# First loads and first products of a fused forward and backward pass, in a new order

## The chip, the cores and the metric

The kernel runs on one core of a Trainium2 chip. The time of a run is what the device takes for one launch, in microseconds (us); a version is given by the median of its runs. A profile is one execution recorded by the hardware profiler, with its own time. The engines are TensorE (PE; its weight loads PEld), VectorE (DVE), ScalarE (ACT), GpSimd (POOL) and SyncE (SP), which here only starts DMA transfers. A name with a q (SPq, ACTq) is the engine's sequencer.

## What is computed

A block with two halves, and the gradients of it: a spectral filter and an MLP, each behind a layer norm that six rows of a condition c scale, shift and gate (sa, ca, ga, sb, cb, gb).

```python
mod = (silu(c) @ w_mod).reshape(1, 6, 1, 1024)      # sa, ca, ga, sb, cb, gb
h = layernorm(x) * (1 + ca) + sa                     # x: 1 x 2048 x 1024, bfloat16
x = x + ga * irfft2(rfft2(h) * (w_r + 1j * w_i))
h = layernorm(x) * (1 + cb) + sb
x = x + gb * (gelu(layernorm(h) @ w1 + b1) @ w2 + b2)   # w1: 1024 x 3584
# outputs: x, and the gradients of x, w_r, w_i, w1, b1, w2, b2, c, w_mod for grad_out
```

## The kernel before

The 2048 tokens are four quarters (blocks) of 512, the 1024 columns eight chunks of 128, the 3584 hidden units 28 chunks of 128 (fc).

**Start.** The rows of the condition come from `mod_block(r, h)`: half a row is eight matmuls (L278) of a broadcast u = silu(c) with a 1024 KB piece of w_mod; `mod_get` loads such a piece from SP (L270) into a ring of three tiles. Row 5 is gb, row 1 ca, row 0 sa; rows 2 to 4 are `late_mods`. grad_out is loaded by quarters (`load_go`, L350). Each quarter of it is transposed by 32 matmuls with an identity (L388), scaled by the gb column (`gb_col`, made by small matmuls at L380) and written to `gBoT[j]` by VectorE (L392) and ScalarE (L396) in turn.

**Products with w2^T.** `load_w2t(fc)` loads a transposed chunk of w2 with a transposing DMA (L341) into one of four slots of `wt`. `ph_part(fc, js)` multiplies it with the quarters js of gBoT: eight matmuls (L814) into one bank for each quarter, a copy (L820) to one of four buffers, and a store to d_ph by POOL (L822) when the fourth quarter is done. All 28 fc are needed before the GELU's backward. The first seven are written ahead of the forward transform (`PH_EARLY` = 6 and one more); the others are written behind it, and the scheduler places them as filling between the transform's matmuls; the last four do their quarters 2 and 3 between the first z blocks.

**x and the folds.** `load_tok` loads a quarter of x so that the transform can fold it by symmetry: half its rows plainly from SP (L143), half by two gathers from POOL (L145). Each quarter is normalised (`ln_dve` for the first, `ln_mix` for the others: statistics on VectorE at L489 and L499 and on ScalarE), scaled by 1 + ca and folded along tokens and columns (`fold_tok`, `fold_d`, `fold_pair`, all through the helper at L194), in the buffer `fbuf`. Quarters 2 and 3 of fbuf first hold quarters 2 and 3 of grad_out.

**Forward transform.** `spectral_core` starts with `s_fwd` (matmuls L538 and L531, `pu`), which needs all four folded quarters and is written behind the last early product (`early_pe`). It multiplies by w_r and w_i in pairs of frequencies (`pair_load`, L557 and L558) and goes back; `consume_fwd` makes the two layer norms and stores n3, the MLP's input, by quarters.

**MLP and backward.** `z_block(b, g)` multiplies n3's quarter b with w1 (L951), evicts on ScalarE (L954) and runs the GELU and its derivative on ScalarE and VectorE, in two sets of temporaries. `plan` writes the order of z blocks, the last products (`p`) and the second MLP product (`bo_pass`), and `ordered()` holds TensorE to it. `pg_pass(b, h)` (L1105) makes the gradient at n3: four banks over seven groups g; ScalarE evicts the banks at L1121. The backward transform follows, with `fill(n)` placing n pieces of the weight gradients (16 matmuls each, L1239 and L1464) between its steps, `halves_sum` for column sums (L217), and `colsum` and `sr` for the sa row's gradient.

**What sets the order.** Each engine runs its instructions in the order that the scheduler wrote at build time, from the program's order and priorities. `tc.issue_after(x)` holds what stands under it behind x in that order. SP and POOL start DMAs in order; a DMA that must wait holds those behind it.

Of the kernel before, what the change touches and what calls it, by code (L numbers as in the profile page):

```python
# [10 lines left out]
FP32 = mybir.dt.float32  # L11
BF16 = mybir.dt.bfloat16
# [5 lines left out]
P = 128  # L18
# [12 lines left out]
NB = 4  # L31
# [4 lines left out]
def kernel(  # L36
# [101 lines left out]
    def tok_idx(i, q):  # L138
        return 1 + q if i % 2 == 0 else 3 * q

    def load_tok(t4, src, i, eng=None):
        s3 = tok_flat(src)
        ins = (eng or nc.sync).dma_start(out=tok_plain(t4, i), in_=tok_rows(s3, i, 0, D))  # L143
        for q in range(2):
            nc.gpsimd.indirect_dma_start(out=t4[:, tok_idx(i, q), :], out_offset=None, in_=s3,  # L145
                                         in_offset=bass.IndirectOffsetOnAxis(ap=xidx[:, 2 * i + q:2 * i + q + 1], axis=0))
        return ins
# [201 lines left out]
    def load_go(j):  # L349
        nc.sync.dma_start(out=gos[j], in_=go_f[j * BW:(j + 1) * BW, :].rearrange("(a p) d -> p a d", p=P))  # L350

# [17 lines left out]
    load_tok(x4s[1], A_x, 1)  # L369
    load_go(2)  # L370
    load_go(3)
    for h in range(2):
        mod_block(5, h, wm[5, h][:])
    load_tok(x4s[2], A_x, 2)
    load_tok(x4s[3], A_x, 3)
    load_w2t(2)
    load_w2t(3)
    pc = ps_d("pc")
    for cch in range(NDC):
        nc.tensor.matmul(pc[:, cch:cch + 1], lhsT=gb_row[0:1, cch * P:(cch + 1) * P], rhs=ones_bf[0:1, 0:1], start=True, stop=True)  # L380
    with tc.high_priority():
        nc.vector.tensor_copy(out=gb_col[:], in_=pc[:, 0:NDC])
    for j in range(4):
        for cch in range(NDC):
            pt = ps_f("pt")
            for a in range(4):
                q = (0, 2, 3, 1)[a] if j % 2 == 0 else (1, 3, 2, 0)[a]
                nc.tensor.matmul(pt[:, q * P:(q + 1) * P], lhsT=gos[j][:, a, cch * P:(cch + 1) * P], rhs=(ident, irev)[a // 2],  # L388
                                 start=True, stop=True)
            if cch % 2 == 0:  # L390
                with tc.high_priority():
                    nc.vector.tensor_scalar(out=gBoT[j][:, cch, :], in0=pt[:], scalar1=gb_col[:, cch:cch + 1], scalar2=0.0,  # L392
                                            op0=ALU.mult, op1=ALU.add, accum_out=gu[:, j, cch:cch + 1])
            else:
                with tc.high_priority():
                    nc.scalar.activation(out=gBoT[j][:, cch, :], in_=pt[:], func=ACT.Identity, scale=gb_col[:, cch:cch + 1],  # L396
                                         accum_out=gu[:, j, cch:cch + 1])

# [54 lines left out]
    def gen_mats():  # L453
# [13 lines left out]
        nc.gpsimd.dma_start(out=d_E[:], in_=em1[:])  # L467

    def ln_act(x4, row, i, jk):
        sv = small.tile([P, 4, 4], FP32, tag="lnsv")  # L470
        for q in range(4):
            nc.scalar.activation(out=jk[:, q, :], in_=x4[:, q, :], func=ACT.Identity, accum_out=sv[:, q, 0:1])
        nc.vector.tensor_scalar(out=sv[:, :, 1:2], in0=sv[:, :, 0:1], scalar1=-1.0 / D, scalar2=None, op0=ALU.mult)
        for q in range(4):
            nc.scalar.activation(out=jk[:, q, :], in_=x4[:, q, :], func=ACT.Square, bias=sv[:, q, 1:2], accum_out=sv[:, q, 2:3])
        ln_fin(sv[:, :, 2:3], sv[:, :, 1:2], sv[:, :, 3:4], 1.0 / D, row, i)

# [66 lines left out]
    def spectral_core(fwd, fb, sms, em, css, pt, evac_u, evac_c, evac_v, consume, o4tag, pfs=None, fill=lambda n: None, mid=lambda: None, beside=lambda n, r_in: None):  # L544
# [7 lines left out]
        def pair_load(n):  # L552
            par, m = n // 4, n % 4
            ws = ws2[:, n % 2]
            for x, w in ((0, A_w_r), (1, A_w_i)):
                sl = w_slot(par, m)
                ld_in[0] = (nc.sync if fwd else nc.gpsimd).dma_start(out=ws[:, x, sl, 0:DF], in_=w_plus(w, par, m))  # L557
# [228 lines left out]

    for h in range(2):
        mod_block(0, h)
    gen_mats()
# [7 lines left out]
    to_cols(b1_col[:], b1r, NFC, ident[:])  # L797
    nc.vector.tensor_scalar(out=sar[:, 0], in0=sar[:, 0], scalar1=8.0, scalar2=None, op0=ALU.mult)
    fold_d(saf.rearrange("p (c d) -> p c d", c=1), sar[:, 0], sar[:, 1])


    pho = reg.tile([P, 3, 4, BW], BF16, name="pho", tag="ot")
    phs = [pho[:, k] for k in range(3)] + [reg.tile([P, 4, BW], BF16, name="phr", tag="ph")[:]]
    last_pe = [None]

    def ordered():
        return tc.issue_after(last_pe[0].ins)

    def ph_part(fc, js):
        ph2 = phs[fc % 4]  # L810
        for j in js:
            pp = ps_f("pp")
            for cch in range(NDC):
                last_pe[0] = nc.tensor.matmul(pp[:], lhsT=wt[:, fc % 4, cch, :], rhs=gBoT[j][:, cch, :],  # L814
                                              start=(cch == 0), stop=(cch == NDC - 1))
            q = (0, 2, 3, 1)[j]
            ov = ph2[:, :, q * P:(q + 1) * P]
            pv = pp[:, :].rearrange("p (i w) -> p i w", w=P)
            with tc.high_priority():
                nc.any.tensor_copy(out=ov, in_=pv)  # L820
        if js[-1] == 3:
            nc.gpsimd.dma_start(out=d_ph[fc * P:(fc + 1) * P, :], in_=ph2.rearrange("p i w -> p (i w)"))  # L822

    PH_EARLY = 6
    late_mods = [(r, h) for r in (2, 3, 4) for h in range(2)]
    for fc in range(PH_EARLY):
        ph_part(fc, (0, 1, 2, 3))
        load_w2t(fc + 4)
        if fc in (3, 5):
            with tc.issue_after(last_pe[0].ins):  # L830
                for r, h in late_mods[3 * (fc // 2 - 1):3 * (fc // 2)]:
                    mod_block(r, h)

    ph_part(PH_EARLY, (0, 1, 2, 3))
    early_pe = last_pe[0]

    for i in range(4):
        x4, fb = x4s[i], fbuf[:, i]
        if i == 0:
            with tc.issue_after(u_in.ins):  # L840
                ln_dve(x4, 0, i)
        elif i > 0:
            ln_mix(x4, 0, i, fb)
        else:
            ln_act(x4, 0, i, fb)
        norm_act(fb, x4, 0, i)
# [49 lines left out]
    PH_KEEP = NFC - 4  # L896
    for fc in range(PH_EARLY + 1, NFC):
# [201 lines left out]
    def pg_pass(b, h, pool, before=lambda: ExitStack()):  # L1099
        pgs = [pool(k)("pg") for k in range(4)]  # L1100
        for g in range(7):
            for i in range(4):
                for k in range(4):
                    with before():
                        last_pg[0] = nc.tensor.matmul(pgs[i][:], lhsT=gzs[b, g][:, k, i * P:(i + 1) * P],  # L1105
                                                      rhs=w1Ts[g][:, k, h * KH:(h + 1) * KH],
                                                      start=(g == 0 and k == 0), stop=(g == 6 and k == 3))
                    last_pe[0] = last_pg[0]
                g0 = 3 if b == NB - 1 else 2
                if b > 0 and h == 0 and (g, i) in ((g0, 0), (g0 + 1, 2), (g0 + 2, 2)):  # L1110
                    for ins in sums_in[g - g0]:
                        behind(ins, last_pg[0])
                    sums_in[g - g0].clear()
            for k in range(4 if b < 2 and h == 1 else 0):
                nc.scalar.activation(out=gzs[b, g][:, k, :], in_=gzs[b, g][:, k, :], func=ACT.Identity,
                                     accum_out=gb1_acc[:, g * 4 + k, b:b + 1])
            if g < 6:
                yield
# [253 lines left out]
    def consume_bwd(i, o4, tmp, tmp2, n1, eb):  # L1372
# [198 lines left out]
```

## Time and profile before

| | |
|---|---|
| median of 3 runs | 1411.57 us (1410.99 to 1412.05) |
| the profiled execution | 1412.42 us |
| its span on the core | 1410.6 us |
| TensorE busy | 1374.2 us |
| VectorE busy | 1072.4 us |
| ScalarE busy | 739.2 us |
| GpSimd busy | 351.2 us |
| granted TensorE clock, mean | 0.992 |
| HBM | 200 GB/s over the span |

The span runs from the first to the last recorded instruction; the rest of the execution's time lies around it. "Busy" is the union of an engine's instructions; a matmul's mean duration is longer than its share of a stream, because matmuls overlap. In a group, the number behind x is the count; "idle before" is the time that the engine stood still just ahead of these instructions, and the name behind the arrow is what ended it.

### The profile page before, as it was taken

Reading aid. Unit: us, or ns where it says so; the run is one execution under the profiler, and the core shown is the slowest. Engines: PE = TensorE matmul, PEld = TensorE weight load, DVE = VectorE, ACT = ScalarE, POOL = GpSimd, SP = SyncE. Lnnn points to the kernel's source line nnn. Section 1 sums busy time; section 2 is a strip of 40 time slices with the busy share of each in tenths; the row PEclk is TensorE's granted clock in tenths of the full one; section 3 lists DMA queues with packets and bytes.
Section 4 is the critical chain, followed back from the end, with each engine's and each line's share of the span. In section 5 each row is a group of like instructions: output and inputs, shape, how many; then the busy total and the mean of one; then the engine's idle time right before and its main releaser. Section 6 shows DMA issues by size and latency. Waiting matters only on the chain. (4 is left out here: it accounts for less than half of the span.)

```text
span 1410.6 us, 18696 instructions
## 1 busy us (share of the span) xinstructions
PE 1374.2 (97%) x6963; PEld 664.5 (47%) x6963; DVE 1072.4 (76%) x1507; ACT 739.2 (52%) x1059; POOL 351.2 (25%) x436
## 2 busy tenths in 40 slices
PE   5998999999999999999999999999999999999999
PEld 2545565444444444444444444444544565444444
DVE  5897889987978777887620688999498757979960
ACT  4774667667877765665314583243622444434311
POOL 5510623201112122112210010112345330322341
PEclk8899999999999999999999999999999999999999
DMA  9972666899787777696999499996689996897971
GB/s 330 301 234 57 176 165 200 265 283 350 256 258 242 229 242 249 189 287 224 298 271 232 138 237 321 259 259 209 197 265 288 261 253 173 218 250 189 286 270 38
DMA packets 361265, 333.22 MB, mean 236 GB/s; under 512 B 208026, under 2 KB 303152, under 8 KB 361046
## 3 DMA queue, kind: packets, MB, share of 16 engines
q1 hardware_dynamic: 319990, 206.01, 55.9%
q0 software_dynamic: 35424, 120.78, 24.5%
q10 hardware_dynamic: 5760, 5.25, 1.2%
q8 instruction: 54, 0.88, 0.3%
q14 instruction: 37, 0.30, 0.1%
HBM read 166.77 MB, written 115.92 MB: 200 GB/s over the span
## 5 line engine op out<-in xcount | busy, mean ns | idle before, releaser
L1105 PE MATMUL pg<-w1T,gzr 128*128 128x512 bf16 x896 | 196.0, 379 | 2.8 <-ACT gn3b L1121 2.8
L814 PE MATMUL pp<-gBoT,wt 128*128 128x512 bf16 x896 | 197.9, 380 | 0.8 <-DVE phr L820 0.4
L1464 PE MATMUL gw1acc<-gzh,n3n 128*128 128x512 bf16 x640 | 140.0, 379 | 0.2 <-DVE gwo L1468 0.2
L1105 PEld LDWEIGHTS <-gzr 128*128 128x128 bf16 x896 | 86.6, 98 | 111.1 <-issue 8.5
L1464 PEld LDWEIGHTS <-n3n 128*128 128x128 bf16 x896 | 87.3, 98 | 107.1 <-issue 3.3
L951 PEld LDWEIGHTS <-w 128*128 128x128 bf16 x896 | 87.2, 98 | 107.0 <-issue 2.5
L814 PEld LDWEIGHTS <-wt 128*128 128x128 bf16 x896 | 87.5, 98 | 104.0 <-issue 1.5
L951 PE MATMUL pz<-n3Tb,w 128*128 128x512 bf16 x448 | 99.2, 379 | 1.0 <-DVE w2sD L1027 1.0
L951 PE MATMUL pz<-n3Ta,w 128*128 128x512 bf16 x448 | 98.7, 379 | 0.0
L1005 PEld LDWEIGHTS <-hhA 128*128 128x128 bf16 x608 | 59.0, 98 | 73.1 <-issue 2.8
L1239 PE MATMUL gw2acc<-gB,hhsA 128*128 128x512 bf16 x416 | 92.2, 379 | 0.0
L954 ACT ACTIVATE gt<-pz,b_col 128x512 bf16<-128x512 f32 x112 | 72.8, 683 | 33.2 <-PE pz L951 33.0
L962 ACT ACTIVATE gt<-gt 128x2048 bf16<-128x2048 bf16 x28 | 53.5, 1911 | 64.8 <-DVE gt L194 64.8
L194 DVE TENSOR_TENSOR gt<-gt,gt 128x2048 bf16<-128x2048 bf16 x56 | 68.6, 1224 | 19.8 <-ACT gt L964 18.5
L194 DVE TENSOR_TENSOR ct<-ct 128x2048 bf16<-128x2048 bf16 x68 | 80.6, 1218 | 0.9
L1468 ACT CAST gwo<-gw1acc 128x512 bf16<-128x512 f32 x50 | 28.4, 581 | 89.3 <-PE gw1acc L1464 78.5
L1247 ACT CAST gwo<-gw2acc 128x512 bf16<-128x512 f32 x40 | 23.3, 584 | 93.6 <-PE gw2acc L1239 90.5
L1239 PEld LDWEIGHTS <-hhsA 128*128 128x128 bf16 x416 | 40.7, 98 | 47.4
L1470 POOL DMA_DIRECT2D out_dram<-gwo x53 | 29.2, 554 | 129.8 <-DVE gwo L1468 67.6
L1464 PE MATMUL gw1acc<-gzu,n3n 128*128 128x512 bf16 x256 | 55.6, 379 | 1.2 <-ACT gwo L1468 1.2
L958 ACT ACTIVATE gt<-gt 128x2048 bf16<-128x2048 bf16 x28 | 53.5, 1909 | 2.1 <-DVE hhC L194 1.3
L964 ACT ACTIVATE gt<-gt 128x2048 bf16<-128x2048 bf16 x28 | 53.4, 1907 | 0.4
(347 smaller groups left out, 2558.4 us busy)
## 6 DMA issues: line engine op xcount, KB each, us to landing
gzr<-d_gz SPq DMA_DIRECT2D x28, 512.0 KB
wblk<-in_w_mod_dram SPq DMA_DIRECT2D x12, 1024.0 KB
out_dram<-otl POOLq DMA_DIRECT2D x48, 256.0 KB, 4.9
d_ph<-pho POOLq DMA_DIRECT2D x21, 512.0 KB, 6.0
d_hh<-hhA POOLq DMA_DIRECT2D x19, 512.0 KB, 5.1
w<-in_B_w_dram SPq DMA_DIRECT2D x7, 1024.0 KB
hhC<-d_ph SPq DMA_DIRECT2D x14, 512.0 KB
w2sA<-d_ph SPq DMA_DIRECT2D x14, 512.0 KB
```

Source lines behind the costliest of these rows:

```text
L194: return nc.vector.tensor_tensor(out=out, in0=a, in1=b, op=op)
L814: last_pe[0] = nc.tensor.matmul(pp[:], lhsT=wt[:, fc % 4, cch, :], rhs=gBoT[j][:, cch, :], start=(cch == 0), stop=(cch == NDC - 1))
L951: last_pe[0] = nc.tensor.matmul(pz[:], lhsT=w1s[g][:, cch, k * P:(k + 1) * P], rhs=n3T[:, cch, :], start=(cch == 0), stop=(cch == NDC - 1))
L954: z_in = nc.scalar.activation(out=zb[:, k, :], in_=pz[:], func=ACT.Identity, bias=b1_col[:, fc:fc + 1], scale=1.0)
L958: nc.scalar.activation(out=av, in_=zb, func=ACT.Square)
L962: nc.scalar.activation(out=sg, in_=bv, func=ACT.Sigmoid, scale=2.0 * GK)
L964: nc.scalar.activation(out=bv, in_=bv, func=ACT.Sigmoid, scale=-2.0 * GK)
L1005: last_pe[0] = nc.tensor.matmul(pbs[i][:], lhsT=hh[:, k, i * P:(i + 1) * P], rhs=wp[:, k, :], start=False, stop=(g == 6 and k == 3))
L1105: last_pg[0] = nc.tensor.matmul(pgs[i][:], lhsT=gzs[b, g][:, k, i * P:(i + 1) * P], rhs=w1Ts[g][:, k, h * KH:(h + 1) * KH], start=(g == 0 ...
L1239: nc.tensor.matmul(acc[:], lhsT=hh_of(fc)[:, t, :], rhs=gBs[t // 4][:, t % 4, h * KH:(h + 1) * KH], start=(t == 0), stop=(t == NT - 1))
L1464: nc.tensor.matmul(acc[:], lhsT=n3ns[t // 4][:, t % 4, cch * P:(cch + 1) * P], rhs=gz2[t // 8][:, t % 8, :], start=(t == 0), stop=(t == NT ...
L1470: eng.dma_start(out=out_4[cch * P:(cch + 1) * P, fg * 512:(fg + 1) * 512], in_=ob)
```

## The change

The order of the first loads, and with it of TensorE's first work, is rewritten:

- gb's two pieces, quarter 0 of grad_out and w2^T 0 and 1 are loaded first; then x0, quarter 1, w2^T 2, ca's pieces, quarter 2, x1, quarter 3, x2, w2^T 3, x3, and behind x3 sa's pieces. Each quarter's gathers of x wait until a named quarter of grad_out has landed.
- Each quarter's transposes are followed at once by its products with fc 0, 1 and 2; the ca row is made behind quarter 1. TensorE's order is written out here.
- `PH_EARLY` is 11: fc 3 to 10 follow, with the rows sa, ga, sb, cb between them, and their copies on ScalarE. The loads of rows 2 to 4 wait for a w2^T load.
- All quarters of x use `ln_mix`, each behind the last evictions of a quarter's transposes. The fold of sa moves into the loop of products.
- The first loads of w_r and w_i wait for w2^T 12.
- In `pg_pass`, for b > 0 and h = 0, the groups are taken in the blocks (0, 1), (2), (3), (4, 5, 6): within a block one bank does all its groups before the next bank.
- In `consume_bwd` one piece of filling moves from behind to ahead of the third column sum. `sr` takes another buffer.

```diff
-    def load_tok(t4, src, i, eng=None):
+    def load_tok(t4, src, i, eng=None, landed=None):
...
-            nc.gpsimd.indirect_dma_start(out=t4[:, tok_idx(i, q), :], out_offset=None, in_=s3,
+            got_ = nc.gpsimd.indirect_dma_start(out=t4[:, tok_idx(i, q), :], out_offset=None, in_=s3,
...
+            if landed is not None:
+                tc.add_manual_dep(got_.ins, landed.ins.name, mybir.DependencyInfo(mybir.DependencyClass.Sync, mybir.DependencyReason.DATA),
+                                  reason="loads in turn")
...
-    mod_get(1, 0)
-    load_tok(x4s[0], A_x, 0)
-    mod_get(1, 1)
     mod_get(5, 0)
-    for h in range(2):
-        mod_block(1, h, wm[1, h][:])
     mod_get(5, 1)
-    load_go(0)
+    go_in = [load_go(0)]
     load_w2t(0)
     load_w2t(1)
-    load_go(1)
-    load_tok(x4s[1], A_x, 1)
-    load_go(2)
-    load_go(3)
+    load_tok(x4s[0], A_x, 0, landed=go_in[0])
+    go_in.append(load_go(1))
+    load_w2t(2)
+    mod_get(1, 0)
+    mod_get(1, 1)
+    go_in.append(load_go(2))
+    load_tok(x4s[1], A_x, 1, landed=go_in[2])
+    go_in.append(load_go(3))
+    load_tok(x4s[2], A_x, 2, landed=go_in[3])
+    load_w2t(3)
+    x3_in = load_tok(x4s[3], A_x, 3, landed=go_in[3])
+    for h in range(2):
+        with tc.issue_after(x3_in.ins):
+            mod_get(0, h)
...
     for h in range(2):
         mod_block(5, h, wm[5, h][:])
-    load_tok(x4s[2], A_x, 2)
-    load_tok(x4s[3], A_x, 3)
-    load_w2t(2)
-    load_w2t(3)
...
+    for j in range(4):
+        turn_go(j)
+        for fc in range(3):
+            ph_part(fc, (j,))
+        if j == 1:
+            for h in range(2):
+                with ordered():
+                    mod_block(1, h, wm[1, h][:])
+    for fc in range(3):
+        load_w2t(fc + 4)
...
-                    ld_in[0] = (nc.sync if fwd else nc.gpsimd).dma_start(out=ws[:, x, sl, 0:DF], in_=w_plus(w, par, m))
+                with tc.issue_after(w2ts[12].ins) if fwd else ExitStack():
+                    ld_in[0] = (nc.sync if fwd else nc.gpsimd).dma_start(out=ws[:, x, sl, 0:DF], in_=w_plus(w, par, m))
...
+                with ordered() if fc < PH_EARLY else ExitStack():
+                    last_pe[0] = nc.tensor.matmul(pp[:], lhsT=wt[:, fc % 4, cch, :], rhs=gBoT[j][:, cch, :],
+                                                  start=(cch == 0), stop=(cch == NDC - 1))
...
-                nc.any.tensor_copy(out=ov, in_=pv)
+                (nc.scalar.copy if 3 <= fc < PH_EARLY else nc.any.tensor_copy)(out=ov, in_=pv)
...
-    PH_EARLY = 6
+    PH_EARLY = 11
...
-    for fc in range(PH_EARLY):
+    for fc in range(3, PH_EARLY):
         ph_part(fc, (0, 1, 2, 3))
+        if fc in (4, 6, 8):
+            with ordered():
+                for r, h in ([(0, 0), (0, 1)], late_mods[0:3], late_mods[3:6])[fc // 2 - 2]:
+                    mod_block(r, h, wm[r, h][:])
         load_w2t(fc + 4)
...
-    ph_part(PH_EARLY, (0, 1, 2, 3))
     early_pe = last_pe[0]
...
-        if i == 0:
-            with tc.issue_after(u_in.ins):
-                ln_dve(x4, 0, i)
-        elif i > 0:
+        dv, ac = turned_in[(0, 2, 3, 3)[i]]
+        with tc.issue_after(dv.ins), tc.issue_after(ac.ins):
             ln_mix(x4, 0, i, fb)
...
-        for g in range(7):
-            for i in range(4):
-                for k in range(4):
+        blocks = ((0, 1), (2,), (3,), (4, 5, 6)) if b > 0 and h == 0 else tuple((g,) for g in range(7))
+        steps = [(g, i, i == 3 and g == block[-1] and block) for block in blocks for i in range(4) for g in block]
+        for n, (g, i, ends) in enumerate(steps):
+            for k in range(4):
...
-        fill((4, 7, 6, 8)[i])
+        fill((4, 7, 7, 8)[i])
         halves_sum(accCA[0], tmp, i == 0, i == 3)
-        fill(2)
+        fill(1 if i == 2 else 2)
...
-    sr = reg.tile([P, 2, 1, D], FP32, name="sr", tag="px0")
+    sr = reg.tile([P, 2, 1, D], FP32, name="sr", tag="smb")
```

More of the change, by code (lines that the diff above doesn't have):

```diff
@@ new lines, with ph_part @@
+    turned_in = []
+    pho = reg.tile([P, 3, 4, BW], BF16, name="pho", tag="ot")
+    phs = [pho[:, k] for k in range(3)]
+    PH_EARLY = 11
+    def ph_part(fc, js):
+        ph2 = phs[fc % 4]
+        for j in js:
+            pp = ps_f("pp")
+            for cch in range(NDC):
+                with ordered() if fc < PH_EARLY else ExitStack():
+                    last_pe[0] = nc.tensor.matmul(pp[:], lhsT=wt[:, fc % 4, cch, :], rhs=gBoT[j][:, cch, :],
+                                                  start=(cch == 0), stop=(cch == NDC - 1))
+            q = (0, 2, 3, 1)[j]
+            ov = ph2[:, :, q * P:(q + 1) * P]
+            pv = pp[:, :].rearrange("p (i w) -> p i w", w=P)
+            with tc.high_priority():
+                (nc.scalar.copy if 3 <= fc < PH_EARLY else nc.any.tensor_copy)(out=ov, in_=pv)
+        if js[-1] == 3:
+            nc.gpsimd.dma_start(out=d_ph[fc * P:(fc + 1) * P, :], in_=ph2.rearrange("p i w -> p (i w)"))
@@ L797, with late_get @@
     to_cols(b1_col[:], b1r, NFC, ident[:])
[L798 to L822, printed above, removed]
-    PH_EARLY = 6
-    late_mods = [(r, h) for r in (2, 3, 4) for h in range(2)]
-    for fc in range(PH_EARLY):
+    phs.append(reg.tile([P, 4, BW], BF16, name="phr", tag="ph")[:])
+    late_mods = [(r, h) for r in (2, 3, 4) for h in range(2)]
+    def late_get(n):
+        for r, h in late_mods[n:n + 3]:
+            with tc.issue_after(w2t_in[0].ins):
+                mod_get(r, h)
+    for fc in range(3, PH_EARLY):
         ph_part(fc, (0, 1, 2, 3))
+        if fc in (4, 6, 8):
+            with ordered():
+                for r, h in ([(0, 0), (0, 1)], late_mods[0:3], late_mods[3:6])[fc // 2 - 2]:
+                    mod_block(r, h, wm[r, h][:])
         load_w2t(fc + 4)
[L829 to L832, printed above, removed]
-    ph_part(PH_EARLY, (0, 1, 2, 3))
+        if fc in (4, 6):
+            late_get(3 * (fc // 2 - 2))
+        if fc == 4:
+            nc.vector.tensor_scalar(out=sar[:, 0], in0=sar[:, 0], scalar1=8.0, scalar2=None, op0=ALU.mult)
+            fold_d(saf.rearrange("p (c d) -> p c d", c=1), sar[:, 0], sar[:, 1])
     early_pe = last_pe[0]
@@ L896 @@
     PH_KEEP = NFC - 4
-    for fc in range(PH_EARLY + 1, NFC):
+    for fc in range(PH_EARLY, NFC):
         if fc >= PH_EARLY + 4:
```

64 lines of the change are left out of this document (30 added, 34 removed).

## The prediction

> **What bounds the kernel now.** The page and the waits of TensorE (engine, line, releaser: us in total, times, longest) come first.
>
> ```profile
> span 1410.6 us, 18696 instructions
> PE 1374.2 (97%) x6963; PEld 664.5 (47%) x6963; DVE 1072.4 (76%) x1507; ACT 739.2 (52%) x1059; POOL 351.2 (25%) x436
> ...
> PE pm L278 <- DMA wblk<-in_w_mod_dram: 9.8, 4, 3.9
> PE pu L538 <- DVE fbuf L194: 5.1, 1, 5.1
> PE pg L1105 <- ACT gn3b L1121: 2.8, 1, 2.8
> ...
> PE accCA L217 <- DVE ct L194: 1.6, 1, 1.6
> ```
>
> TensorE is the bound: its idle time is 1410.6 − 1374.2 = 36.4 us in all, so no reordering can win more than that plus what a slow clock costs. Next, where it idles: the busy time by stretches (PE, PEld, DVE, ACT, POOL with counts; granted clock; DMA share; GB/s).
>
> ```profile
> 0.00:20.00 20.00, 8.73 (x21) 3.05 (x22) 7.76 (x24) 6.57 (x9) 16.54 (x44) 0.97 0.92 324
> 20.00:40.00 20.00, 14.09 (x113) 10.11 (x111) 13.19 (x34) 13.25 (x26) 3.98 (x6) 0.67 1.05 351
> ...
> 2.50:22.50 20.00, 11.04 (x34) 4.09 (x35) 7.88 (x23) 5.28 (x8) 14.62 (x28) 0.91 1.05 371
> 40.50:45.00 4.50, 4.21 (x40) 3.25 (x39) 3.89 (x11) 4.50 (x14) 1.38 (x2) 0.77 1.05 156
> ```
>
> 11.3 + 5.9 = 17.2 us of the 36.4 lie in the first 40 us, while the DMA engines are full. So the start is bound by the order of the bytes, not by work. TensorE's order of time says what it did before the forward transform began (start, duration, count; idle before):
>
> ```profile
> 6.25 3.57 PE L278 MATMUL pm<-wblk,u_b 128*128 128x512 bf16 x8 [3.89 <-DMA wblk<-in_w_mod_dram]
> ...
> 37.05 4.20 PE L388 MATMUL pt<-ident,fbuf 128*128 128x128 bf16 x36 [2.26 <-DMA fbuf<-in_grad_out_dram]
> 41.51 2.55 PE L388 MATMUL pt<-ident,fbuf 128*128 128x128 bf16 x28 [0.27 <-ACT gBoT L396]
> 44.04 5.34 PE L814 MATMUL pp<-gBoT,wt 128*128 128x512 bf16 x24
> ...
> 99.97 7.07 PE L814 MATMUL pp<-gBoT,wt 128*128 128x512 bf16 x32
> ...
> 107.10 9.66 PE L814 MATMUL pp<-gBoT,wt 128*128 128x512 bf16 x44
> 121.87 1.46 PE L538 MATMUL pu<-smA,fbuf 128*128 128x256 bf16 x6 [5.11 <-DVE fbuf L194]
> ...
> 128.06 1.22 PE L538 MATMUL pu<-smA,fbuf 128*128 128x256 bf16 x8
> ```
>
> The forward transform (L538) begins at 121.9. The groups of the stretch 0 to 122 (count | busy, mean ns) give what TensorE had done by then:
>
> ```profile
> L814 PE MATMUL pp<-gBoT,wt 128*128 128x512 bf16 x268 | 59.0, 379 | 0.0
> L278 PE MATMUL pm<-wblk,u_b 128*128 128x512 bf16 x96 | 27.0, 441 | 9.8 <-DMA wblk<-in_w_mod_dram 9.8
> ...
> L388 PE MATMUL pt<-ident,go 128*128 128x128 bf16 x64 | 6.9, 284 | 2.1 <-DVE gBoT L392 1.3 <-DMA go<-in_grad_out_dram 0.7
> ...
> L388 PE MATMUL pt<-ident,fbuf 128*128 128x128 bf16 x64 | 6.7, 284 | 2.6 <-DMA fbuf<-in_grad_out_dram 2.3 <-ACT gBoT L396 0.3
> ```
>
> A warm product costs 7.07/32 = 0.221 us, so 96 modulation products should take 21.2, not 27.0. Useful work is 59.0 + 21.2 + 13.6 = 93.8 us, and 121.9 − 93.8 = 28.1 us are lost before the transform.
>
> **The change, part by part: the start.** It reorders loads and products; it adds no matmul. The sizes and the rate fix when each load lands:
>
> ```profile
> wblk<-in_w_mod_dram SPq DMA_DIRECT2D x9, 1024.0 KB
> x<-in_A_x_dram SPq DMA_DIRECT2D x4, 512.0 KB
> go<-in_grad_out_dram SPq DMA_DIRECT2D x2, 1024.0 KB
> ...
> 31.50 10.70 SPq L341 DMA_TRANSPOSE wt<-in_B_w_dram  x2
> ```
>
> 1024 KB at 371 GB/s is 2.83 us; x is half plain, half gathers, 2.83 together. The two transposed w2 loads that sit at the end of SP's 31.50 to 42.20 are the dip to 156 GB/s in 40.5 to 45.0, so I take 2.25 us for one; from below, a quarter of a wblk's bytes, 0.7; from above half of SP's 10.70, 5.3, which however counts the queue ahead. In the new order: first gb half 6.25 (as the first wblk now), second 9.1, grad_out quarter 0 at 11.9, w2^T 0 and 1 at 16.4, x0 and quarter 1 at 22.1, w2^T 2 at 24.3, the ca row at 30, quarter 2 at 32.8, x1 and quarter 3 at 38.5, then x2, w2^T 3, x3 to 46, the sa row to 52.
>
> TensorE follows, now in one written order. gb row 6.25 + 2 × 3.57 = 13.4, its eviction and the column by about 15 (an estimate: two copies of the 0.7 us kind and some small products). A quarter's 32 transposes take 13.6/4 = 3.4: 18.4. Products 0 and 1 (16 × 0.221 = 3.5) end at 22; product 2 waits for 24.3 and ends at 26.1; quarter 1 (3.4 + 5.3) 34.8; ca row (16 × 0.221) 38.3; quarters 2 and 3 are there, 55.7; products 3 to 10 (256 × 0.221 = 56.6) and eight modulation blocks (8 × 1.77 = 14.2) end at 126.5. By then 352 products are done where 268 were: 84 × 0.221 = 18.6 us more work, 4.6 us later. **TensorE's gain is 14.0 us.** With 0.7 for a transposed load product 2 would wait no more, and it is about 16; with 5.3 the first three land at 22.5 and 33.5, and it is about 5.
>
> [...]
>
> [...]
>
> **The fold chain.** The transform needs all four folded quarters of x. Their cost on VectorE (tile fbuf in 0 to 122; the statistics, two groups), what VectorE evicts, and the chain's end:
>
> ```profile
> 0.00:122.00 122.00, 7.22 (x67) 6.32 (x68) 51.06 (x42) 32.52 (x40) 0.93 0.86 263
> ...
> L499 DVE BATCH_NORM_STATS2 st<-x 128x6 f32<-128x512 bf16 x12 | 7.9, 677 | 0.0
> ...
> L392 DVE TENSOR_SCALAR_CACHE_REDUCE gBoT<-pt,gb_col 128x512 bf16<-128x512 f32 x16 | 11.7, 750 | 3.8 <-PE pt L388 3.3
> ...
> L820 DVE CAST pho<-pp 128x512 bf16<-128x512 f32 x9 | 6.1, 681 | 0.0
> ...
> 121.12 0.69 DVE L194 TENSOR_TENSOR fbuf<-fbuf,sb_saf 128x1024 bf16<-128x1024 bf16 x1
> ```
>
> x and the ca row come later than now, so the chain starts at 38.3. From there: 51.1 of folds, 16 statistics × 0.68 = 10.9, half of the transposes' evictions 5.9, and some 10 of rows, tables and small things (an estimate): 78, to 116, with gaps about 121. The copies of products 3 to 10, part of them VectorE's now, go to ScalarE, which is why this fits. So the written order (126.5) decides. The 5.11 us stop before the transform goes, and with it its cold start: six matmuls took 1.46 (0.243), later eight took 1.22 (0.153); 22 of these are 2.0 us. Against now the transform starts 126.5 − 121.9 = 4.6 later and runs through 2.0 sooner: **2.6 us late**, from −4 (everything lands early) to +14 (the chain waits for all loads to 52 and ends near 136).
>
> Queues: the pair weights' loads, and the sa, ga, sb and cb rows, move behind w2^T loads.
>
> ```profile
> 65.40 0.35 SPq L557 DMA_DIRECT2D ws<-in_A_w_r_dram  x1
> ...
> 100.00:120.00 20.00, 16.76 (x79) 7.48 (x77) 19.83 (x22) 9.49 (x15) 1.06 (x2) 1.00 0.25 80
> ```
>
> The pair loads issue near 105 instead of 65, for work after the transform; the DMA engines are a quarter busy there, so I cost them at nothing. Uncovered, the first two pairs' eight loads of 131 KB are 2.8 us. Three modulation loads are 8.5 us and have two rounds of products, 14.2, above them: nothing; uncovered, up to 8.5. x's gathers now wait on POOL for grad_out to land, the last for quarter 3 at 38.5. Behind them stand the table work (ScalarE's sines wait for it) and the first stores of products, due long after; nothing, as long as the tables are there by the transform. The statistics of x1 wait for quarter 2's evictions and those of x2 and x3 for quarter 3's, near 50, while VectorE has x0 in hand: nothing.
>
> **The first z blocks.** What is late next is the end of the forward stage. TensorE reaches z sooner by its lead of 18.6 us, but ScalarE and VectorE are then still at the last quarter:
>
> ```profile
> 222.32 91.68 PE L814 MATMUL pp<-gBoT,wt 128*128 128x512 bf16 x424
> ...
> 323.03 7.07 PE L951 MATMUL pz<-n3Ta,w 128*128 128x512 bf16 x32
> ...
> 344.26 20.88 PE L951 MATMUL pz<-n3Ta,w 128*128 128x512 bf16 x96
> ...
> 326.95 0.17 DVE L507 TENSOR_SCALAR mv<-mv 128x2 f32<-128x2 f32 x1 [1.46 <-ACT ct L506]
> ...
> 334.41 2.29 DVE L194 TENSOR_TENSOR ct<-ct,rows 128x4096 bf16<-128x4096 bf16 x1 [6.42 <-ACT ct L514]
> ...
> 350.00 2.40 ACT L954 ACTIVATE gt<-pz,b_col 128x512 bf16<-128x512 f32 x4
> ...
> 287.00:345.00 58.00, 57.25 (x266) 25.81 (x264) 44.23 (x71) 38.73 (x51) 5.29 (x9) 1.00 1.02 326
> ```
>
> z(0,1), started at 344.26, is evicted only at 350.00, all four banks in a row, when z(0,2) needs them at 344.26 + 7.07 = 351.3: the slack is under a microsecond. So the lead is worth only what ScalarE and VectorE come earlier. VectorE idles 58 − 44.2 = 13.8 us in 287 to 345; with z(0,0) ready near 305 its GELU can use the 6.4 us gap, the 1.5 us one, and some 1 us of product copies that fell earlier: **9 us**. Bounds: nothing (these queues stay in their order) and 16.6 (every gap, and four copies of 0.7).
>
> **The late edits.** The reordered product pass moves the last three groups of a bank together, so each bank's eviction has 12 matmuls ahead of the next bank's, not 4; this covers the 2.8 us wait behind gn3b: 2.4 (0 to 2.8). One piece moved ahead of the third column sum covers the 1.6 us wait: 1.1 (0 to 1.6); if a wait merely moves to the next bank or piece, both lose as much. The other buffer of sr lies beside the last products: nothing.
>
> **Sum.** −9 + 2.6 − 2.4 − 1.1 = −9.9 us. The profiled execution took 1412.4 with 1.8 around its span of 1410.6; the changed span would be 1400.7, 1402.5 with that. It lies 0.8 above the median 1411.6, so the median becomes **1401.7**.
>
> **Rivals.**
> *Lead survives whole* (0.20). The z stage absorbs it: all gaps are used, the transform begins on time. Then TensorE's own sum decides: −14.0 − 2.0 − 3.5 = −19.5, 1392. For it speaks 13.8 us of idle VectorE; against it the eviction at 350.00.
> *Lead lost* (0.13). No gap is used, −3.5 + 2.6 = about −1, 1411. For it: strict engine queues and slack under 1 us now.
> *Fold chain late* (0.20), the other side. The ca row and x2, x3 land behind everything; the chain starts at about 52, ends near 136, and its lateness passes through to z, where the lead is worth nothing extra. +14 − 2 − 3.5 = +8.5, 1420. It decides once the transform starts more than 9 + 3.5 − 2 = about 10 us late net, so after some 134.
> *It doesn't do what it says* (0.06). DMA is full in both orders; if every transposed load stalls the queue 5.3 us, products wait as now, TensorE's gain is about 5, the transform shifts, and 1411 follows.
>
> **How the numbers follow.** Forecast 0.41, own range 1396 to 1408. Two per mille (2.8 us) is about what this kernel's measurement tells from no change. Faster: 0.40 of the forecast, 0.20, and 0.06 of the 1411 cases: 0.66. Slower: the late chain 0.20 and 0.04 of tails; same 0.10. From 1387 to 1420 leaves out some 0.05 below and 0.12 above.
>
> **What would show it.** First transposes near 15 us and L814 products before 24; 352 products before the first L538; that L538 with no wait on fbuf, at 122 to 130, at full clock; a new wait of TensorE at L951 of some 10 us, released by ScalarE's evictions; gn3b and accCA gone from the waits. Wrong: a wait of L538 on fbuf past 134, or L814 waits on wt in the first 60 us of more than 5 us.

## The result and the profile after

| | before | after |
|---|---|---|
| median | 1411.57 us (1409.44 to 1412.94, 7 runs) | 1422.77 us (1418.23 to 1429.11, 7 runs) |
| ratio to before, 95% interval | | 1.0081 [1.0057, 1.0104] |
| span of the profiled execution | 1410.6 us | 1423.9 us |
| TensorE idle in the span | 36.4 us | 47.8 us |

The change makes the kernel 11.2 us slower; the forecast was 9.9 us faster. In the changed code the w2^T load is L344 and its product L423 (copied at L429), n3's first load L952, the loads of w1 L909, the store of n3 L895, the z block L967 with its eviction L970, the transform L574.

TensorE's waits in the changed kernel (engine, line, releaser: us in total, times, longest):

```profile
PE pp L423 <- DMA wt<-in_B_w_dram: 15.6, 5, 7.9
PE pz L967 <- ACT gt L970: 6.8, 3, 4.5
PE pm L281 <- DMA wblk<-in_w_mod_dram: 3.8, 1, 3.8
PE pp L423 <- DVE pho L429: 3.7, 1, 3.7
PE pg L1122 <- DMA gzr<-d_gz: 3.7, 2, 3.0
```

The old waits on fbuf, gn3b and accCA are gone and those on wblk are shorter. On top stands one that was not there: the products wait for w2^T. Its two long stops, ahead of 24.88 and of 305.24, stand in TensorE's order of time (start, duration, count; idle before):

```profile
24.88 3.59 PE L423 MATMUL pp<-gBoT,wt 128*128 128x512 bf16 x8 [6.44 <-DMA wt<-in_B_w_dram]
...
40.44 1.06 PE L400 MATMUL pt<-ident,fbuf 128*128 128x128 bf16 x16
...
52.94 2.31 PE L400 MATMUL pt<-ident,fbuf 128*128 128x128 bf16 x20 [1.78 <-DVE pho L429]
55.04 6.28 PE L423 MATMUL pp<-gBoT,wt 128*128 128x512 bf16 x24
...
130.63 1.04 PE L574 MATMUL pu<-smA,fbuf 128*128 128x256 bf16 x8
...
305.24 5.72 PE L423 MATMUL pp<-gBoT,wt 128*128 128x512 bf16 x16 [7.86 <-DMA wt<-in_B_w_dram]
...
322.97 7.07 PE L967 MATMUL pz<-n3Ta,w 128*128 128x512 bf16 x32
...
340.68 8.52 PE L423 MATMUL pp<-gBoT,wt 128*128 128x512 bf16 x32 [3.73 <-DVE pho L429]
...
364.45 7.07 PE L967 MATMUL pz<-n3Ta,w 128*128 128x512 bf16 x32 [1.44 <-ACT gt L970]
...
379.87 9.39 PE L967 MATMUL pz<-n3Ta,w 128*128 128x512 bf16 x32 [4.46 <-ACT gt L970]
...
414.31 7.07 PE L967 MATMUL pz<-n3Tb,w 128*128 128x512 bf16 x32
```

The start went much as forecast: the transform begins at 130.6, 4.1 us later than forecast, with no wait, at a granted clock of 1.00, and all 352 early products are done by then. The loss comes later. The first z block of the second quarter (n3Tb) begins at 414.31, where it began before at:

```profile
399.95 7.07 PE L951 MATMUL pz<-n3Tb,w 128*128 128x512 bf16 x32
```

That is 14.4 us late, against a span that is 13.3 us longer: the loss lies between 131 and 414. By stretches (PE, PEld, DVE, ACT, POOL with counts; granted clock; DMA share; GB/s), in the changed kernel:

```profile
250.00:300.00 50.00, 47.38 (x220) 21.26 (x218) 47.15 (x81) 33.45 (x51) 10.87 (x15) 1.00 0.97 237
300.00:350.00 50.00, 39.74 (x165) 16.75 (x166) 32.51 (x47) 24.30 (x32) 3.60 (x6) 0.90 1.06 323
350.00:400.00 50.00, 44.10 (x196) 19.11 (x194) 38.78 (x50) 39.03 (x38) 7.19 (x10) 0.93 0.74 207
```

TensorE idles 2.6 + 10.3 + 5.9 = 18.8 us here, and its granted clock falls to 0.90 and 0.93 (0.63 in the 5.72 us behind the stop of 7.86, 0.75 in the 9.4 behind that of 4.46). VectorE, ScalarE and TensorE are all short of work in 300 to 350 while the DMA engines are full, which points to loads that come late. It is no proof: before, the DMA engines were as full (1.02 in 287 to 345) and TensorE was busy (57.25 of 58 us). SyncE's order there (start, us the issue took, count):

```profile
269.33 0.40 SPq L895 DMA_DIRECT2D d_n<-ct  x1
269.83 2.01 SPq L344 DMA_TRANSPOSE wt<-in_B_w_dram  x1
274.32 11.04 SPq L952 DMA_TRANSPOSE n3Ta<-d_n  x1
285.45 10.30 SPq L344 DMA_TRANSPOSE wt<-in_B_w_dram  x1
295.92 0.67 SPq L909 DMA_DIRECT2D w<-in_B_w_dram  x1
296.68 9.62 SPq L344 DMA_TRANSPOSE wt<-in_B_w_dram  x1
...
311.43 0.53 SPq L895 DMA_DIRECT2D d_n<-ct  x1
```

And in the kernel before:

```profile
262.28 20.73 SPq L341 DMA_TRANSPOSE wt<-in_B_w_dram  x4
283.10 4.87 SPq L936 DMA_TRANSPOSE n3Ta<-d_n  x1
288.13 1.23 SPq L341 DMA_TRANSPOSE wt<-in_B_w_dram  x1
```

n3's load is written behind w2^T 23. TensorE's lead brings w2^T 23 to 269.8, and n3's megabyte with it: from 283 to 274. SyncE spent 11.0 us on it instead of 4.9, and about 10 us on each of the next two w2^T loads, where the one behind it had taken 1.2. Before, TensorE came to product 24 only at about 323.03 − 64 × 0.221 = 308.9 (the first z block less the products ahead of it), some 20 us after its load was started at 288.13. Now it stops for it at 305.24 − 7.86 = 297.4, 12 us after its load was started, and the load lets it go on only 19.8 us after its start (285.45 to 305.24). In this order of VectorE's (idle before in brackets), that engine stops 8.2 us for TensorE's products and then 9.2 us more, because the next store of n3, started at 311.43, stood behind all these loads (started by GpSimd, as in a run below, it goes at 299.6):

```profile
308.87 0.69 DVE L429 CAST pho<-pp 128x512 bf16<-128x512 f32 x1 [8.23 <-PE pp L423]
...
318.79 1.23 DVE L197 TENSOR_TENSOR ct<-ct 128x2048 bf16<-128x2048 bf16 x1 [9.22 <-DMA d_n<-ct]
```

### The profile page after: what moved, and what is told of

It is laid out like the page before. It is cut to its first block, busy times and chain, and to the rows that moved or that the text cites. A ratio compares the mean times of both kernels' runs of the same rounds, so it can differ in the third digit from the quotient of the medians.

```text
span 1423.9 us, 18696 instructions
## 1 busy us (share of the span) xinstructions
PE 1376.1 (97%) x6963; PEld 661.0 (46%) x6963; DVE 1069.4 (75%) x1502; ACT 747.9 (53%) x1071; POOL 351.4 (25%) x436
## 3 DMA queue, kind: packets, MB, share of 16 engines
q0 software_dynamic: 35424, 120.78, 24.9%
## 5 line engine op out<-in xcount | busy, mean ns | idle before, releaser
L423 PE MATMUL pp<-gBoT,wt 128*128 128x512 bf16 x896 | 205.1, 387 | 19.4 <-DMA wt<-in_B_w_dram 15.6
L423 PEld LDWEIGHTS <-wt 128*128 128x128 bf16 x896 | 88.5, 99 | 128.0 <-DMA wt<-in_B_w_dram 18.0
L967 PEld LDWEIGHTS <-w 128*128 128x128 bf16 x896 | 87.7, 98 | 114.9 <-issue 11.8
L967 PE MATMUL pz<-n3Ta,w 128*128 128x512 bf16 x448 | 101.2, 385 | 6.8 <-ACT gt L970 6.8
L967 PE MATMUL pz<-n3Tb,w 128*128 128x512 bf16 x448 | 99.0, 379 | 0.0
L970 ACT ACTIVATE gt<-pz,b_col 128x512 bf16<-128x512 f32 x112 | 72.7, 684 | 34.2 <-PE pz L967 33.8
L978 ACT ACTIVATE gt<-gt 128x2048 bf16<-128x2048 bf16 x28 | 53.5, 1910 | 60.4 <-DVE gt L197 60.4
L197 DVE TENSOR_TENSOR gt<-gt,gt 128x2048 bf16<-128x2048 bf16 x56 | 68.4, 1223 | 16.2 <-ACT gt L980 15.1
L429 ACT CAST pho<-pp 128x512 bf16<-128x512 f32 x62 | 35.2, 582 | 41.2 <-PE pp L423 41.2
L974 ACT ACTIVATE gt<-gt 128x2048 bf16<-128x2048 bf16 x28 | 53.5, 1910 | 5.2 <-DVE w2sA L197 2.3
```

The costliest lines, as they stand in the source:

```text
L197: return nc.vector.tensor_tensor(out=out, in0=a, in1=b, op=op)
L429: (nc.scalar.copy if 3 <= fc < PH_EARLY else nc.any.tensor_copy)(out=ov, in_=pv)
L967: last_pe[0] = nc.tensor.matmul(pz[:], lhsT=w1s[g][:, cch, k * P:(k + 1) * P], rhs=n3T[:, cch, :], start=(cch == 0), stop=(cch == NDC - 1))
L970: z_in = nc.scalar.activation(out=zb[:, k, :], in_=pz[:], func=ACT.Identity, bias=b1_col[:, fc:fc + 1], scale=1.0)
L974: nc.scalar.activation(out=av, in_=zb, func=ACT.Square)
L978: nc.scalar.activation(out=sg, in_=bv, func=ACT.Sigmoid, scale=2.0 * GK)
```

## The experiments

Theory A: the loss is in these loads. Its two forms: the place of n3's load in SyncE's order, or what the DMA engines do for others at that moment. Theory B: the loss is in the new start (transform late, first loads in turn). Theory C: the late edits cost.

**The late edits alone.** The kernel before with the changed `pg_pass`, `fill` and `sr`; and the changed kernel without the new `pg_pass`.

```diff
-        for g in range(7):
-            for i in range(4):
+        blocks = ((0, 1), (2,), (3,), (4, 5, 6)) if b > 0 and h == 0 else tuple((g,) for g in range(7))
...
-        fill((4, 7, 6, 8)[i])
+        fill((4, 7, 7, 8)[i])
```

> The kernel before with the late edits alone (the order of groups in the gradient pass, the moved piece of filling, the other buffer of sr). If the loss is all in the first 420 us, this is 0 to 3.5 us faster than before (the prediction's 2.4 + 1.1): ratio 0.997 to 1.000, with no wait on gn3b or accCA. The rival, that the new order of groups calls for the fifth and sixth group of gz sooner than they land, gives a wait of TensorE on gzr of 3 to 4 us in place of the 2.8 us on gn3b and a ratio of 1.000 to 1.002.

> The changed kernel with the old order of groups in the gradient pass. If the 3.7 us wait on gzr comes from the new order, it goes and a wait on gn3b of 2 to 3 us returns: the time stays within 2 us of the changed kernel's, ratio 1.006 to 1.010. If the wait comes from the shifted loads, it stays beside the gn3b wait and the ratio is 1.009 to 1.012.

Measured: 1407.89 us, ratio 0.9970 [0.9955, 0.9984], and 1425.68 us, 1.0099 [1.0069, 1.0129]. Alone the late edits win about 4.2 us (0.30%), both waits gone; without the new `pg_pass` the changed kernel loses some 3 us more, a difference within the intervals, and a 3.2 us wait for gn3b is back. Theory C falls. The first of the two is the fastest kernel measured here.

**n3's load further back in SyncE's order.** Behind w2^T 25; behind w2^T 27; and behind w2^T 27 with every piece of w1 behind it (n3_27_w1).

```diff
-            with tc.issue_after(w2ts[23].ins) if b == 0 else ExitStack():
+            with tc.issue_after(w2ts[27].ins) if b == 0 else ExitStack():
...
-                for ins in w1_in[:2]:
+                for ins in w1_in:
```

> The changed kernel with one edit: the transposed load of the first quarter of n3 is held behind w2^T 25 instead of 23 on SP. Theory of the SP queue: that load stood at the head of SP before its data was stored, and w2^T 24 and 25 queued behind it and its megabyte; with the edit TensorE's waits on w2^T near 300 (9.2 us) fall under 3, VectorE's two stops of 8 and 9 us at 300 to 319 shrink, and 8 to 12 us come back: ratio 1.000 to 1.003. Rival, the predicted one (the lead is eaten at the first z blocks by ScalarE and VectorE): TensorE's wait only moves to L967 and the ratio stays above 1.006.

> As before, but held behind w2^T 27, the last. Theory of the SP queue: no wait on w2^T near 300 at all, but the load of n3 then issues near 300 and must land before the first z block near 312; a wait of 0 to 4 us on n3 is possible; ratio 0.999 to 1.004. Rival (lead eaten at z): above 1.006.

> The changed kernel, n3's load behind w2^T 27 and all the loads of w1 behind n3's. Theory of the SP queue: the 16.5 us wait on w1 of the run before was w1 0 queued behind four later pieces of w1; it falls to 5 us or less, the first z block starts near 315 instead of 326, and 2 to 8 us more come back: ratio 0.997 to 1.001. Rival (the lead is worth nothing at z, since ScalarE and VectorE are at the last quarter until about 350): the wait only moves to L967 on ScalarE and the ratio stays 1.001 to 1.004.

Measured: 1421.81 us, 1.0074 [1.0051, 1.0098]; 1415.49, 1.0025 [1.0011, 1.0039]; 1410.07, 0.9993 [0.9983, 1.0002]. The first missed: behind w2^T 25 the load took even longer, and w2^T 26 came late instead of 24. SyncE, n3 behind w2^T 25:

```profile
284.05 16.50 SPq L952 DMA_TRANSPOSE n3Ta<-d_n  x1
300.72 1.72 SPq L909 DMA_DIRECT2D w<-in_B_w_dram  x2
302.54 6.32 SPq L344 DMA_TRANSPOSE wt<-in_B_w_dram  x1
```

In the second no w2^T is late, but four pieces of w1 (9.9 us on SyncE) got ahead of n3, and the first z block waits for a piece behind it. TensorE, n3 behind w2^T 27:

```profile
326.50 10.05 PE L967 MATMUL pz<-n3Ta,w 128*128 128x512 bf16 x31 [16.53 <-DMA w<-in_B_w_dram]
```

With both put right, 0.88% or 12.4 us are back. Theory A carries the loss; in which form, the next runs tell.

**Theory B.** The changed kernel with `PH_EARLY` 9, which brings the transform forward; with x's gathers free of their turn; and the mended loads together with 9.

```diff
-    PH_EARLY = 11
+    PH_EARLY = 9
...
-    load_tok(x4s[0], A_x, 0, landed=go_in[0])
+    load_tok(x4s[0], A_x, 0)
```

> The changed kernel with PH_EARLY 9 instead of 11. The fold chain ended at 126.0 and the transform began at 130.6 behind product 10. If VectorE's chain from the folds to the last quarter sets the stage's end, the transform begins near 126 and the time falls by 3 to 6 us against the changed kernel (ratio 1.003 to 1.006). If TensorE's lead sets it, the two products fewer are missing nowhere or cost up to 3 us (ratio 1.008 to 1.011).

> The changed kernel with x's gathers issued freely, not behind the landing of grad_out. If VectorE's late start is what the order of bytes costs, x lands earlier, the fold chain ends before 124, while grad_out's quarters come 2 to 6 us later; the transform, behind product 10, moves by -2 to +3 us and the ratio is 1.006 to 1.011. If the turn of the gathers were what made the loss, the ratio would be under 1.004.

> PH_EARLY 9 and the order of n3_27_w1 together. If the two causes are separate, both gains add: ratio 0.993 to 0.998, as fast as or faster than the kernel before with the late edits alone (0.997). If the fold chain, later than in the kernel before by 4 us, is what stays, 0.997 to 1.001.

Measured: 1427.26, 1.0112 [1.0091, 1.0133]; 1427.86, 1.0110 [1.0078, 1.0142]; 1417.79, 1.0054 [1.0033, 1.0075]. None is faster than the kernel that it starts from. With 9 the transform's matmuls run from 124.3 on, six microseconds sooner, and nothing is won: the loads near 270 to 305 are as slow as before (n3's 8.5 us, then w2^T 11.9 and 12.8). With free gathers TensorE waits 3.1 us for grad_out, and the fold chain ends at 131.7 instead of 126.0: nothing speaks for giving up the turn. The last of the three missed its expectation, which was no difference from the kernel before or a gain; with two chunks' products fewer ahead, the lead is smaller and nine short waits on ScalarE's evictions, 8.7 us in all, come in its place. Theory B falls as the main cause.

**Who holds the DMA engines?** First the traffic by queue (packets, MB, share of the 16 engines, which can add up to more than 100%; q1 is SyncE's, q0 GpSimd's). The changed kernel, 274.3 to 285.4, while n3's load was issued:

```profile
q0 software_dynamic: 425, 1.56, 69.8%
q1 hardware_dynamic: 3213, 0.81, 34.8%
```

The kernel before, 283 to 289, the same load:

```profile
q1 hardware_dynamic: 5148, 1.31, 108.6%
q0 software_dynamic: 75, 0.24, 14.1%
```

Before, GpSimd's gathers and its two 1 MB stores of the third quarter (d_A at 271.7, d_x at 277.7) were all but over when n3's load began at 283.1. Now n3's load is 8.8 us earlier and the stores are 4.7 and 7.5 us later (276.4 and 285.3): the gathers and d_A fall on n3's load, where 69.8% of the engines go to GpSimd, and d_x falls on w2^T 24 behind it. The run that tells place from traffic keeps SyncE's order and moves these stores. Its first version moves those of the wrong quarter:

```diff
-        nc.gpsimd.dma_start(out=chunk_rows(d_A, i), in_=o4)
+        for j in ((0,), (), (1, 2), (3,))[i]:
+            nc.gpsimd.dma_start(out=chunk_rows(d_A, j), in_=o4)
```

> The changed kernel with the two 1 MB stores by GpSimd of the second quarter (d_A and d_x, issued near 276 and 285 us) sent with those of the third quarter, near 338; that quarter is stored from the third quarter's buffers. n3's first load keeps its place behind w2^T 23. If that load and the w2^T behind it are slow because GpSimd's stores take the DMA engines from them (70% of the engines went to GpSimd's queue while n3's load was issued, 35% to SyncE's), SyncE's 11.0 us for n3's load fall to 6 to 8, the 10.3 and 9.6 us of the two w2^T loads behind it to 3 to 6, TensorE's waits for w2^T between 290 and 340 from 9 us to under 4, and 5 to 11 us come back: ratio 1.000 to 1.0045. Rival: the place in SyncE's order is enough by itself (a megabyte of transposed packets ahead of w2^T); then n3's load stays above 9 us, TensorE still waits 7 us or more there, and the ratio is 1.006 or more.

The stores of 276 us are those of the third quarter, not of the second, so this kernel doubled them there (and leaves out the second quarter's own values). Measured: 1429.18 us, 1.0123 [1.0078, 1.0168], some 6 us slower than the changed kernel. n3's load was through in 6.4 us, but the two w2^T behind it then took 13.2 and 16.2 us, and TensorE waited 9.4 and 2.6 us for them. With the right quarter (`((0,), (1,), (), (2, 3))`, for d_x too), which leaves out the third quarter's own values and stores as many bytes:

> The changed kernel with GpSimd's two 1 MB stores of the third quarter (d_A and d_x, at 276 and 285 us) sent with those of the fourth, near 338; the third quarter is stored from the fourth's buffers. SyncE's order stays. If GpSimd's stores take the DMA engines from the transposed loads, SyncE's 11.0 us for n3's load fall to 6 to 8 and the 10.3 and 9.6 us of the two w2^T loads behind it to 3 to 6, TensorE waits under 4 us for w2^T between 290 and 340 instead of 9, and 5 to 11 us come back: ratio 1.000 to 1.0045. Rival: the place of n3's load ahead of w2^T is enough by itself; it stays above 9 us, TensorE waits 7 us or more, and the ratio is 1.006 or more.

Measured: 1411.27 us, 0.9993 [0.9974, 1.0012]. SyncE in it:

```profile
272.87 6.19 SPq L954 DMA_TRANSPOSE n3Ta<-d_n  x1
279.15 8.26 SPq L344 DMA_TRANSPOSE wt<-in_B_w_dram  x1
287.58 0.86 SPq L911 DMA_DIRECT2D w<-in_B_w_dram  x1
288.53 4.35 SPq L344 DMA_TRANSPOSE wt<-in_B_w_dram  x1
```

TensorE's one wait for w2^T left after 290:

```profile
308.21 3.63 PE L423 MATMUL pp<-gBoT,wt 128*128 128x512 bf16 x16 [1.93 <-DMA wt<-in_B_w_dram]
```

SyncE's order is that of the changed kernel, n3's load stands ahead of w2^T 24 to 27, and 11.5 us are back: 6.2 for 11.0, 8.3 and 4.4 for 10.3 and 9.6, and TensorE's waits for w2^T after 290 down from 9.2 to 1.9. So the place alone doesn't make the loss: it takes the place and the traffic of GpSimd's queue at that moment together. Two more runs bear on it: n3's stores started by GpSimd, and the mirror, n3's load behind w2^T 20 in the kernel before.

```diff
-        nc.sync.dma_start(out=chunk_rows(d_n3, i), in_=tmp)
+        nc.gpsimd.dma_start(out=chunk_rows(d_n3, i), in_=tmp)
```

> The changed kernel with the n3 stores started by GpSimd instead of SyncE; n3's first load stays behind w2^T 23. If the stores of the later quarters, queued on SyncE behind that load, are a part of the loss, VectorE's 9.2 us stop on d_n near 318 goes under 2 us, TensorE's 9 us of waits for w2^T near 305 to 312 stay, and 4 to 8 us come back: ratio 1.002 to 1.005. Rival: the w2^T chunks alone set it; the stop on d_n goes but TensorE gains nothing, ratio 1.006 or more.

> The mirror: the kernel before with n3's first load three w2^T chunks earlier on SyncE, behind w2^T 20, nothing else. If the place in SyncE's queue costs by itself, that load stands waiting for its data some 6 to 12 us with w2^T 21 to 23 behind it; TensorE then waits 2 to 6 us on wt ahead of product 21 to 23, and the ratio is 1.001 to 1.005. Rival: the loss in the changed kernel needs TensorE's lead or the traffic of the changed start; then nothing is seen here, ratio 0.999 to 1.001.

Measured: 1433.76 us, 1.0146 [1.0112, 1.0179], a clear miss, and 1414.15, 1.0029 [1.0011, 1.0046]. With n3's stores on GpSimd too, SyncE and TensorE show the worst case of all:

```profile
274.72 31.41 SPq L952 DMA_TRANSPOSE n3Ta<-d_n  x1
306.22 6.82 SPq L344 DMA_TRANSPOSE wt<-in_B_w_dram  x1
```

```profile
323.96 16.95 PE L423 MATMUL pp<-gBoT,wt 128*128 128x512 bf16 x64 [26.67 <-DMA wt<-in_B_w_dram]
```

One load took 31 us. The traffic beside it (275 to 306):

```profile
q1 hardware_dynamic: 2891, 0.74, 57.7%
q0 software_dynamic: 1238, 4.56, 53.3%
```

GpSimd's queue moved 4.56 MB in 31 us, 147 GB/s, hardly more than beside the load in the changed kernel (1.56 MB in 11.1 us, 141 GB/s). But each of SyncE's packets held an engine for some 99 ns (57.7% of 16 engines for 31 us, 2891 packets) where it was 19 ns in the changed kernel and 20 before. So shared engines are not the whole of it: the packets themselves can become slow, and what slows them no run here shows. The stop on d_n went, as expected, but it had been a follower. The mirror's profile shows the load early (265.0, 7.6 us) and no wait of TensorE for w2^T; the 2 to 6 us expected there did not come, and what its 0.29% is made of was not found. It fits that the place costs little where TensorE is not ahead, but shows no more.

**What is left: the start, and the z blocks.** From n3_27_w1: w2^T 2 and quarter 1 ahead of x0 (w2t2_first); then also the first piece of w1 ahead of n3's load.

```diff
+    load_w2t(2)
+    go_in.append(load_go(1))
     load_tok(x4s[0], A_x, 0, landed=go_in[0])
-    go_in.append(load_go(1))
-    load_w2t(2)
...
-                for ins in w1_in:
+                for ins in w1_in[1:]:
```

> n3's first load and the w1 loads as in n3_27_w1 (1410.07 us, ratio 0.9993), and w2^T 2 and quarter 1 are loaded ahead of the first quarter of x. If the start's missing 4 us come from product 2 waiting 6.44 us for w2^T 2 and running cold behind it, that wait falls under 2 us, the quarters end near 57 instead of 61, the transform starts at 126 to 128 instead of 130.6, and the kernel takes 1404 to 1407 us, ratio 0.995 to 0.998. Rival: ScalarE and VectorE set the end of the stage (x and the ca row come no sooner for them, x0 even later); then the wait for w2^T 2 goes as well, but a wait on fbuf of 1 to 4 us or a longer one on gt takes its place, and the ratio stays 0.998 to 1.001.

> w2t2_first (1409.38 us, ratio 0.9986) with the first piece of w1 loaded ahead of n3's first load; only SyncE's order changes. If ScalarE and VectorE set the z blocks, TensorE's 4.5 us wait for w ends (or falls under 2), z(0,0) starts 3 to 5 us sooner, TensorE's waits for gt grow from 5.6 to 8 to 11 us, z(1,0) stays within 1 us of 399.8, and the ratio stays 0.998 to 1.000. Rival: the wait for w was the loss; then z(1,0) comes 3 to 4.5 us sooner, the waits for gt stay near 5.6, and the ratio is 0.9955 to 0.9970.

Measured: 1409.38 us, 0.9986 [0.9972, 0.9999], and 1411.91, 1.0003 [0.9992, 1.0014]. The time of the first lies in its rival's range. The wait for w2^T 2 is gone, but the transposes' waits for VectorE's copies of products grow to 6.6 us (1.8 in the changed kernel); the transform begins at 128.6, and the z blocks are these:

```profile
313.52 9.38 PE L967 MATMUL pz<-n3Ta,w 128*128 128x512 bf16 x32 [4.50 <-DMA w<-in_B_w_dram]
...
365.35 8.75 PE L967 MATMUL pz<-n3Ta,w 128*128 128x512 bf16 x32 [4.03 <-ACT gt L970]
...
389.44 7.07 PE L967 MATMUL pz<-n3Ta,w 128*128 128x512 bf16 x32 [1.53 <-ACT gt L970]
399.80 7.07 PE L967 MATMUL pz<-n3Tb,w 128*128 128x512 bf16 x32
```

In the second:

```profile
310.96 7.07 PE L967 MATMUL pz<-n3Ta,w 128*128 128x512 bf16 x32 [1.48 <-DMA n3Ta<-d_n]
...
365.02 7.07 PE L967 MATMUL pz<-n3Ta,w 128*128 128x512 bf16 x32 [2.81 <-ACT gt L970]
...
399.47 7.07 PE L967 MATMUL pz<-n3Tb,w 128*128 128x512 bf16 x32
```

TensorE is ready for the first z block at 313.52 − 4.50 = 309.0, where before it started it at 323.0: a lead of 14.0 us. At the second quarter it is 0.15 us. Removing the wait for w moves the first z block of the first quarter by 2.6 us (3 to 5 expected) and that of the second by 0.3, while the waits for ScalarE's evictions grow from 5.6 to 8.8 us, in the first and in the second:

```profile
PE pz L967 <- ACT gt L970: 5.6, 2, 4.0
...
PE pz L967 <- ACT gt L970: 8.8, 4, 2.9
```

So the lead isn't lost at the one place that was mended: what TensorE no longer waits for w1 it waits for ScalarE. That ScalarE and VectorE set the pace here is argued from this; no run made them faster.

## Why the prediction was wrong

**The step that failed first** is in the part on the z blocks: "TensorE reaches z sooner by its lead of 18.6 us". It took the last w2^T and n3's load as landed whenever TensorE came for them, and the part on queues priced only the pair, modulation and gather loads. But w2^T loads follow TensorE (a slot must come free), n3's load follows w2^T 23, and GpSimd's stores follow VectorE. TensorE gained on VectorE, so the loads moved into the stores. This term was missing altogether; by two ways of mending it, it is 11.5 us (the moved stores) and 12.7 us (n3's load behind w2^T 27 and ahead of w1), of the 21.1 us between 1401.7 and 1422.77.

**The 9 us at the z blocks** were mis-sized: with the loads mended by SyncE's order, the second quarter's first z block begins at 400.3, 399.8 and 399.5 in the three kernels, and at 399.95 before (402.8 with the moved stores). The gain is nil, the lower bound given, and 1410.07 is 8.4 us above the forecast. The prediction counted VectorE's idle time in 287 to 345 as usable, and its own reading of the eviction at 350.00 (slack under a microsecond) spoke against that. The rival "lead lost", 1411, describes the mended kernels.

**The start's sum** was 4.1 us short: 130.6 for 126.5. Quarters and the ca row ended at 37.0, 40.4, 50.3 and 61.3, where 34.8, 38.3 and, for the last, 55.7 were forecast. w2^T 2 came at 24.9 for 24.3, but the eight products behind the 6.4 us wait ran at a granted clock of 0.50, 3.59 for 1.77, and the transposes of the third and fourth quarters waited for evictions by VectorE, 2.4 + 1.8 us. From there it was 69.3 us instead of 70.8. That 24.3 was so near is luck in part: the first transposes ran at 12.2, not 15, and SyncE spent 7.9 us on w2^T 0 and 1 and 4.4 on w2^T 2, where 2.25 was taken for one. By the prediction's own signs a wait of more than 5 us for w2^T in the first 60 us spoke against it, and this was one. It was not what decided: the kernel with n3's load behind w2^T 27 and ahead of w1 still has that wait, 5.6 us, and is as fast as before; without it, its transform begins at 128.6 instead of 129.7, and the 0.7 us won lie within the interval.

**Right:** the transform's first matmul found its quarters ready, at a granted clock of 1.00; eight took 1.04. The new waits at the z blocks for ScalarE's evictions came, 6.8 us here for "some 10". The fold chain ended at 126.0 for "about 121", still ahead of TensorE. gn3b and accCA are gone, and the late edits win 4.2 us for the 3.5 forecast when alone. In the changed kernel TensorE waits 3.7 us for gzr in the pass one quarter earlier, so less of that is left. The prediction took 5.3 us for a quarter's 24 products right behind its transposes. Behind the third quarter's they took 5.34, 0.223 each, at a granted clock of 1.00, as did the 24 behind 64 transposes in the kernel before (44.04). The fourth quarter's 24, behind a wait of 1.8 us and 20 transposes, took 6.28 at a granted clock of 0.85; no run separates the wait from the transposes there.

**The rivals:** "fold chain late" gave nearly the right time, 1420, by luck: its mechanism did not occur. The right one, a transfer carried by the lead into a busy moment of the DMA engines, was not among them. Not explained: some 2 us of the late edits' gain, which the mended kernels don't show.

## What to carry to other kernels

When an edit makes one engine run ahead, list the loads that are tied to its progress and look at what the other queues move at the time they will now run; the same load can take more than twice as long there (here n3's took 4.9 us on SyncE with 14.1% of the engines on GpSimd's queue, and 11.0 with 69.8%). An engine's lead is worth only what the engines it feeds can take up (here 14.0 us at the first z block, 0.15 at the second quarter's): read their rhythm at the point where it is to be cashed in, and take the lower bound where that point has no slack. The part of a change that wins alone (here 4.2 us) is worth separating from the part that does not.

## What the runs showed of the hardware

Transposed loads: with no other traffic on the engines, in the kernel before (285.3 to 288.3), they moved 0.85 MB in 3.0 us, 283 GB/s, at a share of 124.8%; that kernel's plain first loads and gathers moved 371 GB/s (2.5 to 22.5). Beside GpSimd's gathers and stores 0.81 MB took 11.1 us, 73 GB/s. Their packets are 256 bytes (0.85 MB in 3312), those of GpSimd's queue 3.7 KB on average (1.56 MB in 425). In those 11.1 us GpSimd's 425 packets took 69.8% of the engines and SyncE's 3213 took 34.8%.

SyncE was held from 4.1 us (`PH_EARLY` 9 and the mended loads) to 31.4 (n3's stores on GpSimd) by the first transposed load of n3, the same megabyte. While it was held, its queue moved 0.81 MB in 11.1 us in the changed kernel and 0.74 MB in 31 with n3's stores on GpSimd, so here the load's row on SyncE shows how slowly it got through. What stood behind it waited as long: the next load's row began 0.1 us behind the end of this one, at 285.45 behind 285.36 and at 306.22 behind 306.13.
